# Odd columns of the odd rows from half the table columns, after a turn of the pairs

## The chip, the core and the metric

The kernel runs on one core of a Trainium2 chip. The metric is the device time of one execution in microseconds (us). Three runs of the kernel before gave 1187.96, 1188.49 and 1189.62 us; the median is 1188.49 us. The engines are named as the profile names them: PE is TensorE's matmul, PEld its weight load, DVE is VectorE, ACT is ScalarE, POOL is GpSimd, SP is SyncE, which issues most transfers.

## The reference

```python
x: (8, 3136, 256)      w_in: (256, 1024)   conv_w: (3, 1024)   w_out: (1024, 256)     # float32

X = np.fft.fft(np.fft.fft(x, axis=1), axis=2).real          # FNet mixing: sequence, then features
h = np.maximum(X @ w_in, 0.0)
c = conv_w[0] * h[s-1] + conv_w[1] * h[s] + conv_w[2] * h[s+1]   # along the sequence, zeros outside
out = (h * sigmoid(c)) @ w_out
```

## The kernel before, in words

**The two halves of a batch.** For each of the 8 batches the kernel first makes the Fourier transform along the sequence of the 256 features, as two matrices `PQ[b]` (`pt`, the cosine part, and `qt`, the sine part) of 128 folded features by 1569 frequencies. Then it walks over 32 steps, (chunk of frequencies c, block of 128 hidden features f): 4 chunks by 8 blocks. Over all batches that is 256 steps. The loop at the end of the file is written out by hand as a software pipeline: in cycle t it emits the sigmoid of step t-2, the two products and their copies of step t+1, the sums, seeds and first tap of steps t and t+2, the other taps of step t-1, the gate of step t-2 and the second matrix product of step t-3. Every engine runs its instructions in the order in which they are emitted.

**A step.** `products` (PE, tiles `pb` and `pa`) multiplies `qt` and `pt` with `G`, the input weights that already hold the feature transform. `copies` (ACT, L708) brings `pb` to SBUF, `combine` (DVE, L719) makes sum and difference, `first_tap` (ACT, L725) and `tap` (DVE, L730, twice) are the convolution, `sigmoid` (ACT, L745) and `gate` (half POOL L753, half DVE L754) make the gated rows `g`, and `mm2` (PE, tile `po`) multiplies them with `wout`.

**The transform of the next batch** is slipped into the steps of the present one. It has two kinds of work. `fold_ops(b)` (DVE, L156 to L194, with small copies on POOL, L178) adds and subtracts mirrored rows of `x`, and mirrored features, until four things are left: even and odd frequencies, each for cosine and sine. The result is `wt[b][0]` (even) and `wt[b][1]` (odd), of 98 or 99 partitions by 4 components by 4 row groups q by 128 features. There are 14 such operations in a batch, 7 for each half h of the row groups. `units(b)` then holds nine matrix products against the tables `tabs` (cosine and sine, 393 or 392 frequencies wide): `odd_even` and `odd` for odd frequencies, `even_even` and `even` for even ones, each for sn = 1 (`qt`) and sn = 0 (`pt`), and `feature` for one row in batch 0. A unit is matmuls into one PSUM bank (`pd`, or a spare bank in batch 0), perhaps a copy of it by ACT (`copy`, L294, L324) and sums on DVE (`fin`). `odd` takes row groups 0 and 2, the odd rows: 4 matmuls of 392 columns, no copy, and two sums of 392 elements that read the bank (L340, L342).

**Where things stand.** `side` is a table of extra work by cycle and place ("act", "dve", "pe", "pool", "load"); `at(cycle, where, fn)` fills it. `ends` says until which cycle each batch's folds are spread; the units of batch b follow from `ends[b]` on, and the last folds (batch 7) lie in cycles 157 to 188, the last units in 189 to 220. A unit's `copy` stands in the "act" place of a cycle, which is after `copies` of the next step, and its `fin` in the "dve" place of the same cycle, which is between the two taps.

**The start.** Before the first cycle, batch 0 goes through the same work at once. SP issues the loads of `x`, then the odd tables (`load_tables(1)`, L227 to L233), a quarter of `w_in`, the even tables (`load_tables(0)`), the feature tables `dm` and the rest of `w_in`. PE runs eight products of no use (`keep_on`, into `pb` and `pa`) until the tables are there, then the four odd units of batch 0 in four rounds, part by part. ACT makes the negated tables that the sine terms need (`mirror_tables`, L247) and halves one row (`mend_row`, L241). DVE turns the weights from 64 to 32 bits (`narrow`, L543 to L561).

Of the kernel before, what the change touches and what calls it, by code (L numbers as in the profile page):

```python
# [36 lines left out]
def kernel(  # L37
# [103 lines left out]
    def fold_ops(b):  # L141
# [4 lines left out]
        def half(h):  # L146
# [60 lines left out]
        (o0, s0), (o1, s1) = half(0), half(1)  # L207
        return o0 + o1, {**s0, **{len(o0) + j: f for j, f in s1.items()}}

    tabs = [const.tile([P, n, HQ, HE], F32, name="tab%d" % n) for n in (2, 4)]
    PQ, eb, er = {}, {}, {}
    ed = edp.tile([B, (RC // 2 + 1) * RC], F32, name="ed")

    def table(k, st, q, cols):
        return tabs[st // 2][0:k, st, q, cols] if st < 2 else tabs[1][0:k, st - 2, q, cols]

    def load_tables(par):


        st = slice(2 * par, 2 * par + 2)
        to = tabs[par][:, 0:2].rearrange("p s q i -> p s (q i)")
        n = HQ * HE
        m = NP // 2 // 16 * 16
        for i in range(2):
            nc.sync.dma_start(out=to[i:2 * m:2], in_=dft_seq[0:m, st, HQ * i:HQ * (i + 1)]  # L227
                              .rearrange("p s q i -> p s (q i)"))
        assert NP == 2 * m + 2
        nc.sync.dma_start(out=to[2 * m:NP], in_=bass.AP(  # L230
            tensor=dft_seq.tensor, offset=dft_seq.offset + (m * 4 + 2 * par) * NQ * HE,
            ap=[[n, 2], [NQ * HE, 2], [1, n]]))
        nc.sync.dma_start(out=to[NP:KR], in_=bass.AP(  # L233
            tensor=dft_seq.tensor, offset=dft_seq.offset + ((NP * 4 + 2 * par) * NQ - HQ + 2) * HE,
            ap=[[n, 1], [NQ * HE, 2], [1, n]]))

    def mend_row(par, half):

        for st in range(2):
            row = tabs[par][96:NP, st, HQ - 1]  # L240
            act(row, row, AF.Copy, scale=half[96:NP])  # L241

    def mirror_tables(q):

        for to, of, s in ((2, 1, -1.0), (3, 0, 1.0)):
            for i in range(2):
                act(tabs[1][0:KR, to, q:q + 2, i:HO:2], tabs[1][0:KR, of, q:q + 2, i:HO:2], AF.Copy,  # L247
                    scale=-s if i else s)

    class Unit:  # L250
# [11 lines left out]
        def part(self, i):  # L262
            if i == 0:
                self.p = spare()
            self.mms[i](self.p)

# [13 lines left out]
    def units(b):  # L280
# [34 lines left out]
        def stat(sn):  # L315
            return ((w(4 + 2 * sn), 2 + sn), (w(5 + 2 * sn), 4 + sn))
# [480 lines left out]
    nc.gpsimd.memset(PQ[0][1][96:P, :], 0.0)  # L797
    for f in fold_ops(0)[0]:
        f()
# [49 lines left out]
    def at(cycle, where, fn):  # L849
        side.setdefault((cycle, where), []).append(fn)  # L850
# [57 lines left out]
    for b in range(1, B):  # L908
        ops, singles = fold_ops(b)
        c0, n = ends[b - 1], ends[b] - ends[b - 1]  # L910
        if b == 1:

            cs = [c for c in range(4, ends[1] + 1) if c not in taken]
            assert len(cs) == len(ops) and cs[7] > NF + 4
        else:
            cs = [free(c0 + j * n // len(ops)) for j in range(len(ops))]
            assert cs[-1] < ends[b]
        if b + 1 < B:
            for h in range(2):
                for j, fn in enumerate(load_ops(b + 1, h, nc.sync)):  # L920
                    at(cs[7 * h + 6] + 1 + j, "load", fn)
# [112 lines left out]
```

## Time and profile before

| what | value |
|---|---|
| runs of the kernel before | 1187.96, 1188.49, 1189.62 us |
| span of the profiled execution | 1184.7 us |
| median of the runs less that span | 3.8 us |
| instructions in it | 15354 |

The profile is of one execution. Its span runs from the first instruction of the core to the last one; what lies around it, 3.8 us against the median, is not in the trace, and is taken as the same for both kernels. A row of a group reads: line, engine, operation, tiles out<-in, shapes, count, then busy time and mean duration of one in ns, then the idle time of the engine just before. A float32 matmul stands as two records, so a unit of 4 matmuls shows as x8. On DVE and ACT an instruction's record starts before the one before it has ended, so the distance from start to start, and not the duration, is what one costs when the engine is full.

### The profile page before, as it was taken

How to read it: one execution, taken by the hardware profiler on the slowest of the kernel's cores; microseconds unless marked ns; L12 is line 12 of the kernel's file. 1: busy time of each engine (PE TensorE's matmuls, PEld its weight loads, DVE VectorE, ACT ScalarE, POOL GpSimd, SP SyncE). 2: the span in 40 equal slices, each digit the busy share in tenths (PEclk: the TensorE clock that was granted, in tenths of full speed). 3: DMA queues.
4: the chain of work that ended last, by engine and by line, in shares of the span. 5: the costliest groups of instructions: out<-in, count | busy, mean ns of one | idle time of the engine just before them, and what ended most of it. 6: DMA issues, size and time to landing. Idle time of an engine off the chain costs nothing.

```text
span 1184.7 us, 15354 instructions
## 1 busy us (share of the span) xinstructions
PE 1158.7 (98%) x4820; PEld 891.6 (75%) x4820; DVE 1128.7 (95%) x1633; ACT 886.7 (75%) x1888; POOL 407.6 (34%) x476
## 2 busy tenths in 40 slices
PE   4999999999999999999999999999999999999998
PEld 2667777777777777777777777777777777777776
DVE  7899999999999999999998999999998898999996
ACT  2578668777777778877777877877777777888885
POOL 5225443433434342424333232432322232222222
PEclk9999999999999999999999999999999999999999
DMA  9803233121212021202131110310010100100000
GB/s 226 195 10 107 57 55 89 49 69 41 72 38 86 28 77 52 83 7 76 34 96 46 48 48 14 104 34 27 27 34 21 32 27 27 51 31 27 28 27 32
DMA packets 70068, 66.08 MB, mean 56 GB/s; under 512 B 28107, under 2 KB 57683, under 8 KB 69987
## 3 DMA queue, kind: packets, MB, share of 16 engines
q1 hardware_dynamic: 64349, 51.98, 15.6%
q0 software_dynamic: 5120, 12.85, 3.7%
q8 instruction: 38, 0.62, 0.2%
q14 instruction: 43, 0.35, 0.1%
q10 hardware_dynamic: 518, 0.28, 0.1%
HBM read 39.33 MB, written 25.74 MB: 55 GB/s over the span
## 4 chain that ended last, share of the span: by engine, by line
PE 89%; DVE 7%; issue 1%; POOL 1%; ACT 1%; DMA 0%; DVEq 0%; SPq 0%; POOLq 0%; ACTq 0%
PE po L92 54%; PE pb L92 14%; PE pa L92 13%; PE pd L92 8%; DVE g L730 3%; DVE h L719 1%; DVE g L754 1%; POOL xh L131 1%; DVE raw L558 0%; DVE xh L167 0%; DVE wout L551 0%; ACT os L778 0%; DVE w L194 0%; DVE win L551 0%; DMA out_dram<-os 0%
## 5 line engine op out<-in xcount | busy, mean ns | idle before, releaser
L92 PE MATMUL po<-wout,g 128*128 128x256 f32 x3072 | 706.1, 379 | 4.2 <-DVE g L754 4.2
L92 PEld LDWEIGHTS po<-wout,g 128*128 128x128 f32 x3072 | 580.8, 190 | 148.7 <-issue 20.0
L730 DVE SCALAR_TENSOR_TENSOR g<-h,cw,g 128x770 f32<-128x770 f32 (+1 forms) x512 | 575.7, 1124 | 5.7 <-ACT g L725 2.1
L753 POOL TENSOR_TENSOR g<-g,h 128x385 f32<-128x385 f32 (+2 forms) x256 | 270.4, 1057 | 721.1 <-ACT g L745 542.1
L708 ACT ACTIVATE nb<-pb 128x386 f32<-128x386 f32 (+2 forms) x494 | 219.9, 500 | 168.2 <-PE pb L92 167.5
L745 ACT ACTIVATE g<-g 128x385 f32<-128x385 f32 (+4 forms) x512 | 244.8, 531 | 81.8 <-DVE g L730 78.4
L719 DVE CUSTOM_DVE_ANT_0 h<-pa,nb 128x386 f32<-128x386 f32 (+2 forms) x503 | 260.0, 556 | 2.5 <-POOL h L686 2.5
L725 ACT ACTIVATE g<-h,cw 128x770 f32<-128x770 f32 (+1 forms) x256 | 244.2, 954 | 0.0
L92 PE MATMUL pb<-qt,G 127*128 127x387 f32 (+2 forms) x512 | 213.7, 498 | 0.9 <-ACT G L641 0.9
L92 PE MATMUL pa<-pt,G 128*128 128x387 f32 (+2 forms) x512 | 211.8, 494 | 0.0
L672 ACT ACTIVATE pa<-eb,ge 128x387 f32<-128x387 f32 (+2 forms) x256 | 155.2, 607 | 0.6 <-ACT ft L477 0.6
L92 PEld LDWEIGHTS pa<-pt,G 128*128 128x128 f32 x512 | 96.9, 189 | 73.5 <-issue 18.0
L754 DVE TENSOR_TENSOR g<-g,h 128x385 f32<-128x385 f32 (+2 forms) x256 | 147.7, 577 | 2.4 <-ACT g L745 2.4
L92 PE MATMUL pd<-tab,w 98*128 98x196 f32 (+3 forms) x448 | 115.9, 356 | 0.0
L92 PEld LDWEIGHTS pb<-qt,G 127*128 127x128 f32 x512 | 91.5, 190 | 18.8 <-ACT G L641 1.9
L131 POOL DMA_INDIRECT xh<-in_x_dram,idx x64 | 99.8, 1560 | 13.0 <-issue 10.6
L92 PEld LDWEIGHTS pd<-tab,w 98*128 98x128 f32 (+1 forms) x448 | 82.7, 191 | 12.6
L778 ACT COPY os<-po 128x256 f32<-128x256 f32 x196 | 57.6, 397 | 6.6 <-PE po L92 3.3
L156 DVE TENSOR_TENSOR xh<-xh 98x1020 f32<-98x1020 f32 (+1 forms) x32 | 40.4, 1265 | 2.6 <-DMA xh<-in_x_dram,idx 2.6
L167 DVE TENSOR_TENSOR xh<-xh 98x1024 f32<-98x1024 f32 (+1 forms) x32 | 40.5, 1266 | 0.1
L178 POOL COPY w<-xh 98x4 f32<-98x4 f32 (+1 forms) x32 | 24.2, 758 | 6.1 <-DVE xh L167 3.6
L193 DVE TENSOR_TENSOR w<-xh 98x508 f32<-98x508 f32 (+1 forms) x32 | 23.0, 720 | 0.1
(124 smaller groups left out, 330.3 us busy)
## 6 DMA issues: line engine op xcount, KB each, us to landing
out_dram<-os SPq DMA_DIRECT2D x192, 128.0 KB
xh<-in_x_dram SPq DMA_DIRECT2D x16, 784.0 KB
eb<-ed SPq DMA_DIRECT2D x16, 193.5 KB
tab<-dft_seq_dram SPq DMA_DIRECT2D x4, 589.5 KB
raw<-in_moe_w_in_dram SPq DMA_DIRECT2D x4, 512.0 KB
raw<-in_moe_w_out_dram SPq DMA_DIRECT2D x1, 2048.0 KB
eb<-ed SPq DMA_DIRECT2D x8, 209.0 KB
eb<-ed SPq DMA_DIRECT2D x7, 193.0 KB
```

The costliest lines, as they stand in the source:

```text
L92: nc.tensor.matmul(o, l, r, start=start, stop=stop, skip_group_check=True)
L131: nc.gpsimd.indirect_dma_start(out=xh[b, h][0:NP, 7 - m].rearrange("p q d -> p (q d)"), out_offset=None, in_=bass.AP(tensor=x.tensor, offs ...
L167: vt(flat(to, to + 2), flat(0, 2), flat(2, 4), op=op)
L672: act(pa[s][:, 0:n], eb[b, c], AF.Copy, scale=ge[:, f:f + 1])
L708: act(nb[s][:, i, cols], p[:, cols], AF.Copy, scale=-1.0 if i else 1.0)
L719: nc.vector._custom_dve(TENSOR_ADD_SAT, out=to, in0=a[:, cols], in1=c[:, i, cols], s0=BIG, s1=0.0)
L725: act(gs[s], hs[s][:, 0:n], AF.Copy, scale=cw[:, 0, s[2]:s[2] + 1])
L730: stt(out=g, in0=h[:, k:k + n], scalar=cw[:, k, f:f + 1], in1=g, op0=ALU.mult, op1=ALU.add)
L745: act(gs[s][:, c], gs[s][:, c], AF.Sigmoid)
L753: gt(g[:, p], g[:, p], h[:, p], op=ALU.mult)
L754: vt(g[:, v], g[:, v], h[:, v], op=ALU.mult)
L778: nc.scalar.copy(out=osb[:, j % 2], in_=pt[:, j % 2])
```

## The change

The units `odd` no longer multiply with the 392 columns of the odd tables. An odd frequency is 4j+1 or 4j-1, so the rows are first turned, pair by pair, by the angle of frequency 1; after that both frequencies come from the products at frequency 4j, as sum and difference of the cosine part and the sine part. So a unit makes 197 columns of each part, side by side in one bank, with every second column of the even tables, and the sums follow.

- **The turn.** In batches 1 to 7, two ACT operations for each half copy the two sides of the odd rows of `wt[b][1]` with the sine as scale (`scaled`, tile `rt`, 98 partitions by 256), and two DVE operations turn them in place (`turned`, 98 by 256). They are one more fold operation for each half: 16 in a batch, and `ends[1]` goes from 20 to 22. In batch 0 ACT makes four scaled copies for each half (8 in all), and the unit adds them up with 8 matmuls.
- **The unit.** 4 matmuls of 197 columns (8 in batch 0) in place of 4 of 392. ACT copies one half of the bank (`copy`, 197 columns). DVE makes two more sums of 196 elements into an SBUF tile, and the two sums of 392 now read that tile and not the bank.
- **The tables.** Of the odd tables only row groups 1 and 3 at 196 columns are loaded (`load_odd`, 8 transfers with rows of 784 bytes, in place of 4 with rows of 6288 bytes), then the even tables (`load_even`), and only after these the first quarter of `w_in`. `load_turn` (4 transfers of single elements on ACT's queue) brings the cosines and sines of the turn. `mirror_tables` is 4 ACT operations of 196 elements, where it was 8 of 392.

```diff
@@ fold_ops, half(h)
+            def sides():
+                w = wt[b][1][0:NP, :, 2 * h]
+                return w[:, 0:4:2], w[:, 1:4:2]
+            made = []
+            def scaled():
+                if b == 0:
+                    a, c = sides()
+                    for i, (v, k) in enumerate(((a, 0), (c, 2), (a, 1), (c, 0))):
+                        if i % 2 == 0:
+                            parted[h, i // 2] = rp.tile([P, 2, 2, P], F32, name="rt", tag="rt")
+                        act(parted[h, i // 2][0:NP, i % 2], v, AF.Copy, scale=turn[0:NP, k, h:h + 1])
+                    return
+                made.append(rp.tile([P, 2, 2, P], F32, name="rt", tag="rt"))
+                for i, v in enumerate(sides()):
+                    act(made[0][0:NP, i], v, AF.Copy, scale=turn[0:NP, 1, h:h + 1])
+            def turned():
+                if b == 0:
+                    return
+                for i, v in enumerate(sides()):
+                    stt(out=v, in0=v, scalar=turn[0:NP, 0, h:h + 1], in1=made[0][0:NP, 1 - i],
+                        op0=ALU.mult, op1=ALU.add if i else ALU.subtract)
-            ops = [pair(0), pair(2), both(6, ALU.subtract), feats(1), both(4, ALU.add), evens, feats(0)]
-            return ops, {3: single(1), 6: single(0)}
+            ops = [pair(0), pair(2), both(6, ALU.subtract), feats(1), both(4, ALU.add), turned, evens, feats(0)]
+            return ops, {3: single(1), 7: single(0)}, {5: scaled}
@@ tables
-    tabs = [const.tile([P, n, HQ, HE], F32, name="tab%d" % n) for n in (2, 4)]
+    tabs = [const.tile([P, 2, HQ, HE], F32, name="tab2"), const.tile([P, 4, 2, QO], F32, name="tab4")]
+    turn = const.tile([P, 3, 2], F32, name="turn")
+    rp = ctx.enter_context(tc.tile_pool(name="rp", bufs=4))
+    def load_odd(eng):
+        def at_(p, s, q):
+            return dft_seq.offset + ((p * 4 + 2 + s) * NQ + q) * HE
+        for s in range(2):
+            for i in range(2):
+                eng.dma_start(out=tabs[1][i:2 * MR:2, s], in_=bass.AP(
+                    tensor=dft_seq.tensor, offset=at_(0, s, HQ * i + 1),
+                    ap=[[4 * NQ * HE, MR], [2 * HE, 2], [1, QO]]))
...
@@ units, odd(sn)
-            prods = [(q, wf, st) for q in (0, 2) for wf, st in stat(sn)]
-            mms = [product((slice(0, P), slice(0, HO)), wf, st, q, slice(0, HO), i == 0, i == 3)
-                   for i, (q, wf, st) in enumerate(prods)]
+            n = HE // 2 + 1
+            def from_(i, e):
+                if b == 0:
+                    return lambda k, q: parted[q // 2, i ^ sn][0:k, e, sn, :]
+                return w(4 + 2 * sn + (i ^ sn))
+            m = 1 if b else 2
+            mms = [product((slice(0, P), slice(i * n, (i + 1) * n)), from_(i, e), i, q,
+                           slice(0, HE, 2), i + q + e == 0, q == 2 and e == m - 1)
+                   for q in (0, 2) for i in range(2) for e in range(m)]
+            def copy(p):
+                a_["s", sn], a_["b", sn] = [asp.tile([P, HO + 2], F32, name="as", tag="as") for _ in range(2)]
+                nc.scalar.copy(out=a_["s", sn][:, 0:n], in_=p[:, n:2 * n])
             def fin(p):
-                a, bb, t = a_[sn][:, 0:HO], p[:, 0:HO], PQ[b][sn]
+                a, t = a_[sn][:, 0:HO], PQ[b][sn]
+                u, v, bb = p[:, 0:n], a_["s", sn][:, 0:n], a_["b", sn][:, 0:HO]
+                if sn:
+                    vt(bb[:, 0:HO:2], v[:, 0:n - 1], u[:, 0:n - 1], op=ALU.add)
+                    vt(bb[:, 1:HO:2], v[:, 1:n], u[:, 1:n], op=ALU.subtract)
+                else:
+                    vt(bb[:, 0:HO:2], u[:, 0:n - 1], v[:, 0:n - 1], op=ALU.subtract)
+                    vt(bb[:, 1:HO:2], u[:, 1:n], v[:, 1:n], op=ALU.add)
                 vt(t[:, 1:Q4 + 1:2], a, bb, op=ALU.add)
                 x0, x1 = (bb, a) if sn else (a, bb)
                 vt(t[:, M - 1:Q4:-2], x0, x1, op=ALU.subtract)
-            return Unit(b, mms, lambda p: None, fin)
+            return Unit(b, mms, copy, fin)
@@ the start
+    load_turn(nc.scalar)
+    act(turn[0:NP, 2], turn[0:NP, 1], AF.Copy, scale=-1.0)
     nc.gpsimd.memset(tabs[1][0:1, 0, 0, 0:1], 0.0)
-    load_tables(1)
+    load_odd(nc.sync)
+    load_even()
     w_in[0].load(nc.sync)
-    load_tables(0)
     nc.sync.dma_start(out=dm, in_=dft_dim[:, :, 0:2])
...
-    mirror_tables(0)
     mend_row(1, half)
-    mirror_tables(2)
+    mirror_tables()
@@ the schedule
-    ends = [9, 20, per + 12] + [per * (b - 1) - 3 + max(11 - 4 * (b - 2), 0) for b in range(3, B)]
+    ends = [9, 22, per + 12] + [per * (b - 1) - 3 + max(11 - 4 * (b - 2), 0) for b in range(3, B)]
...
+        for j, fn in pres.items():
+            at(cs[j], "act", fn)
```

More of the change, by code (lines that the diff above doesn't have):

```diff
@@ L202, in feats @@
                 return f
[L204 to L212 removed]
+            def sides():
[21 more added lines that the diff above has]
+            return ops, {3: single(1), 7: single(0)}, {5: scaled}
+        parts = [half(h) for h in range(2)]
+        n = len(parts[0][0])
+        return (parts[0][0] + parts[1][0],
+                *[{n * h + j: f for h in range(2) for j, f in parts[h][i].items()} for i in (1, 2)])
+    parted = {}
+    tabs = [const.tile([P, 2, HQ, HE], F32, name="tab2"), const.tile([P, 4, 2, QO], F32, name="tab4")]
+    turn = const.tile([P, 3, 2], F32, name="turn")
+    rp = ctx.enter_context(tc.tile_pool(name="rp", bufs=4))
     PQ, eb, er = {}, {}, {}
@@ L216, in table, with load_even @@
     def table(k, st, q, cols):
[L217 to L223, printed above, removed]
+        if st < 2:
+            return tabs[0][0:k, st, q, cols]
+        return tabs[1][0:k, st - 2, q // 2, cols]
+    MR = NP // 2 // 16 * 16
+    assert NP == 2 * MR + 2
+    def load_even():
+        to = tabs[0].rearrange("p s q i -> p s (q i)")
@@ L237, in mend_row, with load_turn @@
+    def load_turn(eng):
+        for s in range(2):
+            for i in range(2):
+                eng.dma_start(out=turn[i:NP:2, s].unsqueeze(2), in_=bass.AP(
+                    tensor=dft_seq.tensor, offset=dft_seq.offset + ((2 + s) * NQ + HQ * i) * HE,
+                    ap=[[4 * NQ * HE, NP // 2], [2 * HE, 2], [1, 1]]))
     def mend_row(par, half):
         for st in range(2):
-            row = tabs[par][96:NP, st, HQ - 1]
+            row = tabs[0][96:NP, st, HQ - 1] if par == 0 else tabs[1][96:NP, st, 1]
@@ L264, in part @@
                 self.p = spare()
-            self.mms[i](self.p)
+            n = len(self.mms) // 4
+            for f in self.mms[i * n:(i + 1) * n]:
+                f(self.p)
         def copy(self):
@@ L797 @@
     nc.gpsimd.memset(PQ[0][1][96:P, :], 0.0)
-    for f in fold_ops(0)[0]:
+    ops, _, pres = fold_ops(0)
+    for j, f in enumerate(ops):
+        if j in pres:
+            pres[j]()
         f()
@@ L908 @@
     for b in range(1, B):
[L909 removed]
+        ops, singles, pres = fold_ops(b)
         c0, n = ends[b - 1], ends[b] - ends[b - 1]
@@ L913 @@
             cs = [c for c in range(4, ends[1] + 1) if c not in taken]
-            assert len(cs) == len(ops) and cs[7] > NF + 4
+            assert len(cs) == len(ops) and cs[len(ops) // 2] > NF + 4
         else:
@@ L920 @@
                 for j, fn in enumerate(load_ops(b + 1, h, nc.sync)):
-                    at(cs[7 * h + 6] + 1 + j, "load", fn)
+                    at(cs[len(ops) // 2 * (h + 1) - 1] + 1 + j, "load", fn)
         for j, fn in enumerate(ops):
```

18 lines of the change are left out of this document (10 added, 8 removed).

## The prediction

> **What bounds the kernel now.** I read the page first: its busy line, then its chain of work that ended last.
>
> ```profile
> PE 1158.7 (98%) x4820; PEld 891.6 (75%) x4820; DVE 1128.7 (95%) x1633; ACT 886.7 (75%) x1888; POOL 407.6 (34%) x476
> ...
> PE 89%; DVE 7%; issue 1%; POOL 1%; ACT 1%; DMA 0%; DVEq 0%; SPq 0%; POOLq 0%; ACTq 0%
> ```
>
> TensorE is the bound, but VectorE is three points behind it, and the change takes work from the one and gives some to the other. A mean over the span can't decide that, so the next view is the windows, with columns for PE, PEld, DVE, ACT and POOL. I cut them where the work changes: 60 to 160 (folds of batch 1), 160 to 880 (folds of batches 2 to 7), 880 to 1025 (units of batch 7 alone), the rest (neither).
>
> ```profile
> 60.00:160.00 100.00, 96.81 (x400) 71.77 (x399) 99.38 (x149) 74.20 (x169) 40.31 (x49) 1.00 0.28 60
> 160.00:400.00 240.00, 239.37 (x1000) 183.81 (x999) 235.69 (x345) 181.72 (x387) 95.41 (x107) 1.00 0.21 61
> 400.00:880.00 480.00, 479.58 (x2005) 373.02 (x2004) 466.85 (x688) 370.92 (x778) 164.44 (x189) 1.00 0.15 48
> 880.00:1025.00 145.00, 145.00 (x608) 113.22 (x607) 131.16 (x184) 111.03 (x239) 40.65 (x41) 1.00 0.10 31
> 1025.00:1150.00 125.00, 125.00 (x514) 97.11 (x513) 123.94 (x161) 104.45 (x221) 31.64 (x40) 1.00 0.09 30
> ```
>
> In the first window VectorE bounds (99.38 of 100, PE 96.81). From 160 to 1150 TensorE is never idle for more than 0.7 us in a window. VectorE's idle time is 4.3 us in the second window and 13.2 in the third. The last row warns: there VectorE has neither folds nor units and still shows 99%. Its busy time stretches, which the taps show, same shape, in 100 to 160, 160 to 400, 400 to 880 and 1030 to 1150 (count, busy us, mean ns):
>
> ```profile
> L730 DVE SCALAR_TENSOR_TENSOR g<-h,cw,g 128x770 f32<-128x770 f32 x26 | 26.5, 1018 | 0.0
> L730 DVE SCALAR_TENSOR_TENSOR g<-h,cw,g 128x770 f32<-128x770 f32 x75 | 79.7, 1062 | 0.3
> L730 DVE SCALAR_TENSOR_TENSOR g<-h,cw,g 128x770 f32<-128x770 f32 x169 | 182.8, 1082 | 0.8
> ...
> L730 DVE SCALAR_TENSOR_TENSOR g<-h,cw,g 128x770 f32<-128x770 f32 x48 | 58.5, 1218 | 0.8
> ```
>
> The more room VectorE has, the longer a tap: 1018 ns where VectorE bounds, 1218 where it has least to do. So part of VectorE's busy time is slack, and it goes when VectorE gets tight. That decides this case.
>
> **What TensorE saves.** The timeline of PE has a whole `odd` unit of today, and an `even` unit of 197 columns with every second column of a table, just the form that `odd` gets:
>
> ```profile
> 141.04 2.80 PE L92 MATMUL pd<-tab,w 98*128 98x392 f32 x8
> 143.68 0.81 PE L92 MATMUL pb<-qt,G 127*128 127x387 f32 x2
> ...
> 156.38 1.56 PE L92 MATMUL pd<-tab,w 98*128 98x197 f32 x8
> 157.78 0.87 PE L92 MATMUL pb<-qt,G 127*128 127x418 f32 x2
> ```
>
> From start to next start: 143.68 - 141.04 = 2.64 us before, 157.78 - 156.38 = 1.40 after. Saved are 1.24 us a unit, 2.48 a batch, 17.4 us over 14 units of batches 1 to 7. In batch 0 there are 8 matmuls: 2.80 against 2.64, 0.16 more for each of two units.
>
> **What VectorE gets.** Sums of 196 elements with one input in PSUM exist; turns of 256 elements don't, but one operation of their kind of 128 elements and one of 512 do.
>
> ```profile
> 948.45 0.36 DVE L300 TENSOR_TENSOR as<-pd,as 128x196 f32<-128x196 f32 x1
> 948.73 1.01 DVE L730 SCALAR_TENSOR_TENSOR g<-h,cw,g 128x770 f32<-128x770 f32 x1
> ```
>
> ```profile
> 5.83 0.28 DVE L561 SCALAR_TENSOR_TENSOR cw<-raw,cw 24x128 f32<-24x128 f32 x1
> ...
> 60.33 0.69 DVE L561 SCALAR_TENSOR_TENSOR wout<-raw,wout 128x512 f32<-128x512 f32 x1
> ```
>
> A sum costs 948.73 - 948.45 = 0.28 us from start to start. A turn lasts between 0.28 and 0.69, by the straight line 0.42; less the 0.08 by which such records overlap it is 0.34, and with a scalar from memory a little more: I take 0.38. A batch has 4 turns and 4 new sums: 1.5 + 1.1 = 2.6 us. The two sums of 392 remain as they are; only their second input moves from PSUM to SBUF.
>
> **What that makes of each window.** By the cycles of the schedule, 400 to 880 holds 3.7 batches of turns and 3.8 pairs of odd units, 160 to 400 2.3 and 1.7, 60 to 160 1 and 0.5, 880 to 1025 none and 1.
>
> *400 to 880.* TensorE: -3.8 x 2.48 = -9.4, so 470.6. VectorE: 466.9 + 3.7 x 1.5 + 3.8 x 1.1 = 476.6 busy as it stands; but if its 225 taps (the 169 of the row and the wider ones of every fourth chunk, taken alike) go back from 1082 to 1018 ns, 14.4 us go: 462.2. That leaves 8.4 us of idle time, where it has 13.2 now. TensorE remains the bound if VectorE's waits shrink. I take 2.4 us off for places where they don't: **-7**. *160 to 400.* TensorE 240 - 1.7 x 2.48 = 235.8; VectorE 235.7 + 2.3 x 1.5 + 1.7 x 1.1 = 241.0, less 44 ns (1062 - 1018) on half as many taps is 236.1. Both bound; with 1.4 us of idle time it is 237.5: **-2.5**. *60 to 160.* VectorE bounds, so its additions count in full, 1.5 + 0.6: **+2.1**, and TensorE's saving is lost. *880 to 1025.* No folds; one batch of odd units, VectorE has 14 us: TensorE's 2.5, **-2.4**. *After that* nothing changes: 0.
>
> What else hides: ACT gets 4 scaled copies and 2 bank copies a batch.
>
> ```profile
> L294 ACT COPY as<-pd 128x197 f32<-128x197 f32 x14 | 4.6, 331 | 0.0
> L247 ACT ACTIVATE tab<-tab 99x392 f32<-99x392 f32 x8 | 3.9, 573 | 15.5 <-DMA tab<-dft_seq_dram 15.5
> ```
>
> Between 0.33 (197) and 0.57 (392) a copy of 256 is 0.40, so 4 x 0.40 + 2 x 0.33 = 2.3 us on an engine that is 75% busy: nothing by itself, but DVE waits for each result, and the seed and first tap stand behind them in ACT's queue. POOL and the steady transfers are unchanged.
>
> Some of the stretch comes from POOL, as the timeline shows at one place: two taps and a gate of POOL that start together, and an undisturbed gate.
>
> ```profile
> 603.87 2.79 DVE L730 SCALAR_TENSOR_TENSOR g<-h,cw,g 128x832 f32<-128x832 f32 x2
> 603.88 1.90 POOL L753 TENSOR_TENSOR g<-g,h 128x448 f32<-128x448 f32 x1 [3.50 <-ACT g L745]
> ...
> 607.40 0.98 POOL L753 TENSOR_TENSOR g<-g,h 128x448 f32<-128x448 f32 x1 [1.62 <-ACT g L745]
> ```
>
> The gate takes 1.90 where it takes 0.98 alone. [...]
>
> **The start.** SP's issues, ACT's first use of the odd tables, PE's change from idle products to the odd units, and DVE's first sum:
>
> ```profile
> 13.41 1.40 SPq L227 DMA_DIRECT2D tab<-dft_seq_dram  x2
> 14.86 0.44 SPq L230 DMA_DIRECT2D tab<-dft_seq_dram  x1
> 15.34 0.68 SPq L233 DMA_DIRECT2D tab<-dft_seq_dram  x1
> ```
>
> ```profile
> 22.52 1.97 ACT L247 ACTIVATE tab<-tab 99x392 f32<-99x392 f32 x4 [15.46 <-DMA tab<-dft_seq_dram]
> ```
>
> ```profile
> 24.00 1.88 PE L92 MATMUL pa<-w 98*128 98x512 f32 x4
> 25.72 2.48 PE L92 MATMUL po<-tab,w 98*128 98x196 f32 x10
> ```
>
> ```profile
> 32.55 0.36 DVE L328 TENSOR_TENSOR as<-as,po 128x196 f32<-128x196 f32 x1 [2.42 <-ACT as L324]
> ```
>
> Loading a quarter of the odd tables gains nothing, for `odd` now needs the even ones, which are issued behind eight small transfers: 2 x 1.40 + 2 x 0.44 + 2 x 0.68 = 5.0 us, so from 18.4 to 20.9. Today the last odd table is issued by 16.0 and used at 22.52, 6.5 later: the even ones land at 27.4 by that, and no later, since part of these 6.5 us was `x` still loading. The idle products hold PE until 25.72 in any case. So the odd units start between 0 and 1.7 us late; I take 0.7. Then come 0.3 us of matmuls in batch 0 and four new sums on DVE, 1.1 us, in a row that is unbroken from the first sum on. A quarter of `w_in` lands later, but DVE idles 2.42 us ahead of 32.55, which covers it. **+2**, between 1.1 and 3.5.
>
> **Sum:** +2 + 2.1 - 2.5 - 7 - 2.4 = -7.8. Span 1184.7 - 7.8 = 1176.9. The median of the runs, 1188.49, is 3.8 us over the profiled span, so 1180.7 us.
>
> **Rivals.**
>
> *A: VectorE becomes the bound from 60 to 880, through its waits for ACT (slower).* A unit's bank copy stands in ACT's queue behind `copies` of the next step, which waits for PE. The waits of 400 to 900, in total us, times, longest:
>
> ```profile
> DVE as L328 <- ACT as L324: 5.2, 5, 2.1
> DVE as L298 <- ACT as L294: 4.8, 8, 1.1
> ```
>
> 10.0 us for 13 waits, 0.77 each. The change adds four such waits a batch (two turns, two odd units): 15 x 0.77 = 11.6 us in 400 to 880, 8 x 0.77 = 6.2 in 160 to 400. If the old and the new ones all stay, 400 to 880 is 462.2 + 13.2 + 11.6 = 487 (+7), 160 to 400 is 236.1 + 4.3 + 6.2 = 246.6 (+6.6), and the sum is +2 + 2.1 + 6.6 + 7 - 2.4 = +15.3, so 1203.8 us. These are 35.3 us of waits, of which the forecast keeps 12.2; the kernel turns slower than before from the point where 7.8 of the other 23.1 stay, a third. Against it speaks a window in which VectorE bounds today:
>
> ```profile
> 220.00:240.00 20.00, 19.49 (x79) 14.94 (x80) 19.93 (x31) 15.00 (x31) 5.37 (x10) 1.00 0.01 4
> ```
>
> VectorE's idle time there is 0.07 us: where PE isn't late, ACT isn't either. But no unit lies in it. Chance 0.20.
>
> *B: it evens out.* The stretch of the taps goes only half: 400 to 880 is 462.2 + 7.2 + 10.8 = 480.2, 160 to 400 236.1 + 2.5 + 1.4 = 240.0, and the sum is +2 + 2.1 + 0 + 0.2 - 2.4 = +1.9; with somewhat fewer waits 0: 1188.5 to 1190.4. For it: in 160 to 400, with VectorE at 98%, taps still take 1062. Chance 0.16.
>
> *C: nearly all of TensorE's saving arrives.* 160 to 400 -4.2, 400 to 880 -9.4, start +1.1: with +2.1 and -2.4 the sum is -12.9, 1175.6. Chance 0.18.
>
> *D: the halved columns don't halve the time.* If a record of 197 columns cost what a weight load does (891.6 us for 4820, 185 ns, so 1.48 for eight), 14 x 0.08 = 1.1 us of the saving would go. The row at 156.38 has the very form at 1.40: inside the forecast.
>
> **How the numbers follow.** Forecast 0.46 (1177 to 1185), C 0.18, B 0.16, A 0.20. Two tenths of a per cent, 2.4 us, is what a measurement of this kernel can tell from no change. Faster: forecast, C and a little of B, 0.66. Within: most of B and the lowest part of A, 0.14. Slower: the rest of A, and of B, 0.20. The range takes in C and the lower half of A: 1174 to 1196.
>
> **What would show each step.** The `pd` unit of 197 columns with `w` of the odd half at 1.40 us from start to start; turns near 0.38; PE with idle time in 60 to 160 and 160 to 400, and next to none in 400 to 880; mean tap of 400 to 880 near 1020 to 1040; `po<-tab` of the odd units starting between 25.7 and 27.4; stages after 1025 as long as before. It is wrong if DVE's waits for `as` and `rt` in 400 to 880 exceed 12 us, or the taps stay at 1080 there, or the start is over 4 us late.

## The result, and the profile after

| | time, median (range) | span of the profiled execution, granted clock |
|---|---|---|
| before, 5 runs | 1188.04 us (1185.01 to 1189.62) | 1184.7 us, 0.998 |
| changed kernel, 5 runs | 1200.36 us (1193.45 to 1201.21) | 1193.2 us, 0.995 (a run of 1194.98) |

The ratio is 1.0089 with a 95% interval of 1.0063 to 1.0115. The kernel became slower where 1180.7 us was forecast, and lies above the range, 1174 to 1196. Its runs are 7.8 us apart, and they go with the granted clock: 1193.45 and 1194.98 had 0.997 and 0.995, the other three 0.988 to 0.990. That belongs to the result, as the start below shows.

From the page of the changed kernel, the busy line and the chain of work that ended last:

```profile
PE 1152.5 (97%) x4836; PEld 890.9 (75%) x4836; DVE 1134.9 (95%) x1693; ACT 899.6 (75%) x1937; POOL 405.5 (34%) x476
...
PE 72%; DVE 16%; issue 4%; ACT 4%; DMA 2%; POOL 1%; SPq 0%; DVEq 0%; ACTq 0%; POOLq 0%
```

TensorE is 6 us less busy, though the odd units alone save 17. VectorE is 6 us busier. TensorE's share of the chain fell from 89 to 72%, VectorE's rose from 7 to 16%: the bound has moved towards VectorE. The windows of the prediction:

```profile
60.00:160.00 100.00, 94.33 (x388) 69.65 (x389) 96.17 (x143) 76.73 (x175) 47.25 (x45) 1.00 0.30 54
160.00:400.00 240.00, 234.73 (x985) 178.51 (x985) 235.41 (x361) 178.93 (x385) 92.87 (x106) 1.00 0.22 61
400.00:880.00 480.00, 477.56 (x2022) 373.43 (x2020) 472.04 (x722) 379.47 (x809) 159.89 (x189) 1.00 0.16 50
880.00:1025.00 145.00, 145.00 (x617) 114.32 (x616) 133.64 (x195) 113.62 (x242) 39.25 (x44) 1.00 0.09 29
1025.00:1150.00 125.00, 125.00 (x516) 97.32 (x515) 123.41 (x163) 105.22 (x224) 30.82 (x39) 1.00 0.11 32
```

TensorE, idle 0.6 us from 160 to 400 and 0.4 from 400 to 880 before, is now idle 5.3 and 2.4. From 880 on it is full again. What it waits for, from 60 to 880 (us in total, times, longest), first of the matmuls, then of the weight loads, then of the weight loads of the kernel before:

```profile
PE po L92 <- DVE g L830: 10.2, 22, 1.2
```

```profile
PEld po L92 <- DVE g L830: 47.3, 79, 1.8
```

```profile
PEld po L92 <- DVE g L754: 15.6, 24, 1.5
```

The second product waits for the last operation of VectorE's step three times as often as before. So VectorE now bounds a part of this stretch. It isn't full either: from 160 to 880 it is idle for 12.5 us and TensorE for 7.7, each waiting at times for the other.

Stages can be compared without fixed windows by the start of the first matmul of `mm2` (`po<-wout,g`) of a step. How much later it comes than in the profile of the kernel before, and what was forecast for the stretch from the row above to this one:

| step | before, us | after, us | later by | of it in this stretch | forecast |
|---|---|---|---|---|---|
| 0 | 63.0 | 71.0 | +8.0 | +8.0 | +2 |
| 24 | 180.1 | 189.8 | +9.8 | +1.8 | +2.1 |
| 72 | 394.6 | 408.2 | +13.6 | +3.8 | -2.5 |
| 184 | 883.7 | 894.6 | +10.9 | -2.7 | -7 |
| 216 | 1025.2 | 1033.6 | +8.4 | -2.5 | -2.4 |
| 240 | | | +8.4 | 0 | 0 |

Two places failed: the start, and the steps 24 to 184, where -9.5 was forecast and +1.1 came.

**The start.** SP's issues, PE and ACT of the changed kernel:

```profile
13.49 1.37 SPq L274 DMA_DIRECT2D tab<-dft_seq_dram  x2
15.31 0.70 SPq L277 DMA_DIRECT2D tab<-dft_seq_dram  x1
16.06 0.61 SPq L279 DMA_DIRECT2D tab<-dft_seq_dram  x1
18.12 1.27 SPq L274 DMA_DIRECT2D tab<-dft_seq_dram  x2
...
22.59 0.62 SPq L264 DMA_DIRECT2D tab<-dft_seq_dram  x1
```

```profile
25.84 0.49 PE L92 MATMUL po<-tab,w 98*128 98x196 f32 x2
29.90 1.65 PE L92 MATMUL po<-tab,rt 98*128 98x197 f32 x4 [3.56 <-DMA tab<-dft_seq_dram]
...
35.49 0.86 PE L92 MATMUL po<-tab,rt 98*128 98x197 f32 x4
...
42.79 0.88 PE L92 MATMUL pd<-tab,ea 99*1 99x197 f32 x16 [2.29 <-issue]
```

```profile
41.73 0.33 ACT L403 COPY as<-po 128x197 f32<-128x197 f32 x1 [1.51 <-DVE qt L416]
42.08 1.13 ACT L294 ACTIVATE tab<-tab,half 2x393 f32<-2x393 f32 x2
```

```profile
SPq L274 <- DMA tab<-dft_seq_dram: 1.4, 1, 1.4
```

SP stands still between 16.67 and 18.12; the waits of SP give the reason, the landing of an earlier table. So the last even table is issued at 23.2, not 20.9. It is used 6.7 us later, which is the 6.5 of the prediction. So PE, which had begun the odd units at 25.84, waits 3.56 us for the even tables. It waits a second time, 2.29 us, ahead of the feature unit: that needs the halved row of the even tables (L294), which stands in ACT's queue behind the odd units' bank copies, and the last of these waits 1.51 us for a buffer (`as`) that VectorE frees.

In the first gap, 1.9 us after it began, the granted clock falls. The window 30 to 35 of the changed kernel has PEclk 0.50, where before it is 1.00:

```profile
30.00:35.00 5.00, 5.00 (x16) 5.00 (x17) 3.50 (x7) 0.00 (x0) 0.00 (x0) 0.50 0.97 352
```

In all, the clock is at half for 6.8 us from 28.2 and 3.4 us from 52.1; before, only for 3.4 from 42.3, with no gap of TensorE over 0.5 us in the 26 us ahead of it. A round of four records takes 1.65 us at half clock (29.90) and 0.86 at full (35.49). The gap need not be 3.56 us long: in two runs below rounds at half clock (1.65 and 1.52 us) also follow the first gap, which is 2.87 us in e6 and 1.99 in e4. After the 1.19 us of e9 the rounds take 0.86.

### The profile page after: what moved, and what is told of

Its sections match the earlier page's. It is cut to its first block, busy times and chain, and to the rows that moved or that the text cites. A ratio compares the mean times of both kernels' runs of the same rounds, so it can differ in the third digit from the quotient of the medians.

```text
span 1193.2 us, 15532 instructions
## 1 busy us (share of the span) xinstructions
PE 1152.5 (97%) x4836; PEld 890.9 (75%) x4836; DVE 1134.9 (95%) x1693; ACT 899.6 (75%) x1937; POOL 405.5 (34%) x476
## 4 chain that ended last, share of the span: by engine, by line
PE 72%; DVE 16%; issue 4%; ACT 4%; DMA 2%; POOL 1%; SPq 0%; DVEq 0%; ACTq 0%; POOLq 0%
PE po L92 46%; PE pb L92 11%; PE pa L92 10%; DVE g L806 7%; PE pd L92 5%; DVE h L795 3%; DVE g L830 2%; POOL xh L131 1%; DMA tab<-dft_seq_dram 1%; ACT nb L784 1%; ACT g L821 1%; DMA out_dram<-os 1%; ACT os L854 1%; DVE w L194 1%; DMA xh<-in_x_dram 0%
## 5 line engine op out<-in xcount | busy, mean ns | idle before, releaser
L806 DVE SCALAR_TENSOR_TENSOR g<-h,cw,g 128x770 f32<-128x770 f32 (+1 forms) x512 | 564.8, 1103 | 4.1 <-ACT g L801 0.9
L829 POOL TENSOR_TENSOR g<-g,h 128x385 f32<-128x385 f32 (+2 forms) x256 | 265.1, 1036 | 727.5 <-ACT g L821 550.2
L92 PE MATMUL pd<-tab,w 98*128 98x197 f32 (+2 forms) x448 | 98.5, 318 | 1.0 <-DVE w L194 1.0
L178 POOL COPY w<-xh 98x4 f32<-98x4 f32 (+1 forms) x32 | 26.9, 842 | 7.3 <-DVE xh L172 3.7
```

The source lines that it names most:

```text
L92: nc.tensor.matmul(o, l, r, start=start, stop=stop, skip_group_check=True)
L806: stt(out=g, in0=h[:, k:k + n], scalar=cw[:, k, f:f + 1], in1=g, op0=ALU.mult, op1=ALU.add)
L829: gt(g[:, p], g[:, p], h[:, p], op=ALU.mult)
```

## The experiments

Each row gives the time, its ratio to the kernel before on the same chip, and from the profile the lateness of step 0 and what the stretch from step 24 to step 184 gained (-) or lost (+) against the kernel before.

| run | time, us | ratio [95%] | step 0 | 24 to 184 |
|---|---|---|---|---|
| changed kernel | 1200.36 | 1.0089 [1.0063, 1.0115] | +8.0 | +1.1 |
| e1 even tables first | 1194.85 | 1.0067 [1.0053, 1.0081] | +8.2 | +0.6 |
| e2 PE kept busy | 1195.98 | 1.0072 [1.0059, 1.0086] | +5.2 | 0.0 |
| e9 start reordered | 1189.73 | 1.0017 [1.0008, 1.0025] | +1.8 | +0.8 |
| e3 no turn | 1190.59 | 1.0013 [0.9997, 1.0029] | +13.6 | -4.5 |
| e4 no sums | 1186.48 | 0.9991 [0.9981, 1.0] | +5.7 | -4.6 |
| e5 neither | 1179.85 | 0.993 [0.9918, 0.9942] | +6.5 | -8.4 |
| e6 scaled copies early | 1197.04 | 1.0059 [1.0037, 1.0082] | +13.5 | -1.6 |
| e7 POOL 5/8 of the gate | 1227.41 | 1.0309 [1.0284, 1.0334] | +14.6 | +23.3 |
| e10 e9, POOL 3/8 | 1192.0 | 1.0038 [1.0024, 1.0052] | +2.3 | +2.1 |
| e11 before, POOL 3/8 | 1188.62 | 1.0009 [1.0, 1.0018] | -0.1 | 0.0 |
| e12 e9 and e6 | 1186.24 | 0.9992 [0.9983, 1.0001] | +3.4 | -1.0 |
| e13 e12, bank copies first | 1181.04 | 0.9937 [0.9923, 0.995] | +2.2 | -5.9 |
| e14 before, bank copies first | 1189.25 | 1.0005 [0.9996, 1.0014] | +0.4 | +1.0 |

The same steps 24 to 184 in the changed kernel, e1, e2 and e9, whose edits touch only the start, spread from 0.0 to 1.1; that is the grain of the last column.

### The start: e1, e2, e9

e1 issues the even tables ahead of the odd ones.

```diff
-    nc.gpsimd.memset(tabs[1][0:1, 0, 0, 0:1], 0.0)
-    load_odd(nc.sync)
+    nc.gpsimd.memset(tabs[0][0:1, 0, 0, 0:1], 0.0)
     load_even()
+    load_odd(nc.sync)
```

> The changed kernel, with the even tables issued ahead of the eight small transfers of the odd ones. Theory S (most of the loss is the start: the odd units of batch 0 wait for the even tables, which are issued late): the first second matrix product (po<-wout) starts at 63 to 66 us instead of 71.0, the odd units of batch 0 start near 25.8 instead of 29.9, PE has no idle gap there and no stretch at half clock between 28 and 35 us, and the time is 5 to 9 us under that of the changed kernel, so 1186 to 1193. Rival V (the loss is VectorE's load in the steps, the start is only moved slack): the time stays within 2 us of 1195 to 1200.

PE in e1:

```profile
26.30 0.57 PE L92 MATMUL po<-tab,w 98*128 98x196 f32 x2 [1.02 <-DMA tab<-dft_seq_dram]
...
37.14 0.88 PE L92 MATMUL pd<-tab,ea 99*1 99x197 f32 x16 [2.33 <-ACT tab L294]
37.95 9.03 PE L92 MATMUL po<-tab,w 99*128 99x99 f32 x32
```

The late tables are gone: the odd units start at 26.30, at full clock, and the feature unit 5.7 us earlier than in the changed kernel. Yet step 0 comes as late as there. After the idle 2.33 us the clock falls to half for 17.1 us, from 37.9 on, and the even units take 9.03 us where they take 4.85. The miss shows that the clock is a cost of its own.

e2 leaves the loads and has PE run four more idle products ahead of the odd units.

```diff
+    keep_on([idle] * 4)
```

> The changed kernel, with four more idle products on PE ahead of the odd units of batch 0, so that PE is busy while it waits for the even tables; loads as they are. If the granted clock falls to a half because PE sat idle 3.6 us (26.3 to 29.9), the clock stays whole through the odd units of batch 0, which then take 8 us instead of 10.6, and the first second matrix product starts 3 to 4 us earlier, at 67 to 68 us. If the half clock has another cause, or the delay is only that of the tables, it starts at 71 as before. Rival V: no change in the time beyond 2 us either way.

In the profiled run (1191.13 us) the clock is whole through the odd units, and step 0 comes 5.2 us late in place of 8.0. So 6.8 us of half clock cost 2.8 us, 0.41 us each. The other runs, at clocks of 0.992 to 0.994, took 1195.2 to 1196.4. The second gap, ahead of the feature unit, is still there, and e1 shows what can follow it; no trace of these slower runs exists.

e9 is e1 with the halving of the row moved ahead of the odd units.

```diff
     mirror_tables()
+    mend_row(0, half)
     for i in range(4):
...
-    mend_row(0, half)
```

> The start alone, put in another order: even tables before the odd ones (as in the run before), and the halving of the even tables' row ahead of the odd units in ACT's queue, so that the feature unit does not wait behind the odd units' copies. Theory C (the start cost 8 us: some 2.6 of work, some 2.6 of late tables, the rest by TensorE's idle times and the half clock that follows them): TensorE's idle time before the feature unit shrinks from 2.3 us to under 1, no half clock longer than 3.4 us follows, the first mm2 of step 0 comes 2 to 4 us after that of the kernel before, in place of 8, and the time is 1188 to 1191. Rival N (the start's loss is the work itself, the clock no more than a companion): step 0 comes 6 us or more late again, 1193 or more.

```profile
26.17 0.57 PE L92 MATMUL po<-tab,w 98*128 98x196 f32 x2 [1.19 <-DMA tab<-dft_seq_dram]
...
34.61 0.87 PE L92 MATMUL pd<-tab,ea 99*1 99x197 f32 x16
35.41 4.85 PE L92 MATMUL po<-tab,w 99*128 99x99 f32 x32
...
43.40 1.05 PE L92 MATMUL po<-dm,win 128*128 128x1 f32 x6 [1.80 <-DVE win L635]
```

The gap ahead of the odd units is 1.19 us in place of 3.56, and the one ahead of the feature unit is gone. A later one of 1.80 us has come, for VectorE's conversion of the weights. The half clock is 3.4 us, as before. Step 0 comes 1.8 us late, and the time is 1189.73 us; each against the kernel before on its chip, that is 9 to 10 us less than the changed kernel. So in this order the change costs the start 1.8 us; the order that it came with costs the rest. How much that is depends on the clock: 6.2 us in the profiled run of the changed kernel; the profile of e6 below, which has the same start, shows 6.8 and then 17.1 us of half clock and step 0 at +13.5, at a granted clock of 0.990, which is that of the changed kernel's slower runs. None of these was profiled, so for the median this is likely and not shown.

### What VectorE got: e3, e4, e5

e3 leaves out the turn in batches 1 to 7, scaled copies and VectorE's operations; e4 the two new sums and the bank copy of each odd unit, so that the sums of 392 read the bank; e5 both.

```diff
@@ e3: scaled(), turned()
+                if b:
+                    return
...
-                if b == 0:
-                    return
+                return
@@ e4: copy(p), fin(p) of odd
-                nc.scalar.copy(out=a_["s", sn][:, 0:n], in_=p[:, n:2 * n])
+                pass
...
-                u, v, bb = p[:, 0:n], a_["s", sn][:, 0:n], a_["b", sn][:, 0:HO]
+                a, t, bb = a_[sn][:, 0:HO], PQ[b][sn], p[:, 0:HO]
```

> The changed kernel with the turn left out in batches 1 to 7: neither ACT's scaled copies nor VectorE's turns run there (the odd frequencies of these batches are not those of the reference). Theory V (VectorE has no room between 60 and 880 us): 28 turns of some 0.40 us are 11 us less on VectorE, and the time falls by 5 to 10 us; steps 24 to 184 take 4 to 9 us less. Rival (TensorE bounds, the turns are hidden): less than 2 us. Rival A (the waits for ACT's results cost the time): 5 us, the 4.9 us that VectorE waits for rt.

> The changed kernel with the two new sums of each odd unit and ACT's copy of half the bank left out, in all batches; the sums of 392 read the bank as it stands (the odd frequencies are not those of the reference). Theory V: 28 sums of 0.28 us are 8 us less on VectorE in the steps and 1 us less in the start, and the time falls by 4 to 8 us. Rival (TensorE bounds): less than 2 us, all of it in the start.

> The changed kernel without the turn of batches 1 to 7 (its ACT copies and DVE operations) and without the two new sums and the bank copy of each odd unit: both parts are left out, so that only TensorE's halved columns remain. Theory V (VectorE bounds 160 to 880, so what VectorE gets counts in full there): from the first mm2 of step 24 to that of step 184 the changed kernel lost 1.1 us, without the turn it gained 4.5, without the sums 4.6; the two add up, so without both it gains 9.5 to 11.5. Rival S (VectorE's instructions stretch, and either part alone already gives back what there is): no more than 6. Rival W (TensorE's saving is smaller than its columns say): no more than 6 too, but then DVE has idle time there and TensorE none. If V and the start costs what it did in the four runs so far (5 to 8): 1181 to 1185 us.

Against +1.1, the turn costs 5.6 us between step 24 and step 184 and the sums 5.7; together 9.5. Rows of the changed kernel, 400 to 880, give the sizes:

```profile
L226 DVE SCALAR_TENSOR_TENSOR w<-w,turn,rt 98x256 f32<-98x256 f32 x16 | 7.0, 482 | 2.4 <-ACT rt L220 2.4
...
L409 DVE TENSOR_TENSOR as<-as,pd 128x196 f32<-128x196 f32 x4 | 1.4, 357 | 0.3 <-ACT as L403 0.2
L410 DVE TENSOR_TENSOR as<-as,pd 128x196 f32<-128x196 f32 x4 | 1.4, 352 | 0.0
```

Less 0.08 us of overlap, a turn costs 0.40 (0.38 was taken) and a sum 0.28 (0.28). With the prediction's 6 batches of turns and 5.5 of odd units from 160 to 880 that is 6 x 4 x 0.40 = 9.6 us and 5.5 x 4 x 0.28 = 6.2. Left out alone, they give 5.6 and 5.7 us back, and left out together 9.5 of the 15.8 us. So what VectorE gets counts for the greater part, and not in full. The stretch with neither is -8.4, not the -13.6 of TensorE alone (5.5 pairs of units by 2.48); e5 expected 9.5 to 11.5. Halved columns, not missing work, are all that is left in e5, but VectorE still waits for ACT's bank copies of the other units (160 to 880):

```profile
DVE as L354 <- ACT as L350: 6.7, 10, 0.9
DVE as L384 <- ACT as L380: 5.3, 7, 1.2
```

That made me try the waits.

### The waits: e6, e12, e13, e14

VectorE's waits in the changed kernel, 60 to 890:

```profile
DVE w L226 <- ACT rt L220: 4.9, 11, 2.0
DVE as L383 <- ACT as L379: 2.3, 3, 1.1
...
DVE as L412 <- ACT as L403: 1.3, 2, 0.8
DVE as L409 <- ACT as L403: 0.8, 2, 0.5
```

In the kernel before, over the same stretch:

```profile
DVE as L298 <- ACT as L294: 7.1, 11, 1.1
DVE as L328 <- ACT as L324: 6.5, 8, 2.1
```

9.3 us, against 13.6 before. At first I took them for harmless. e6 puts the scaled copies one fold operation earlier in ACT's queue.

```diff
-            ... {5: scaled}
+            ... {4 if b else 5: scaled}
```

> The scaled copies of the turn stand one fold operation earlier in ACT's queue in batches 1 to 7, so that DVE has them long before it turns. Theory V: DVE waited for them only 4.9 us in all, in 11 waits, and part of that is hidden: step 24 to step 184 within 1.5 us of the changed kernel, and the time within 2 us of it at the same granted clock. Rival A of the prediction (the new waits are the loss): the stretch gets shorter by 4 us or more.

VectorE's wait for `rt` goes to nothing, and the stretch is 2.7 us shorter: more than the 1.5 that I allowed and less than rival A's 4. e12 repeats it on e9's start, and there it is 1.8 us (+0.8 to -1.0).

> The reordered start, and the scaled copies of the turn one fold operation earlier. Alone, the earlier copies made 24 to 184 2.7 us shorter and DVE's waits for them went from 2.9 us to 0. With the start, step 0 comes 1.8 us after that of the kernel before, 24 to 184 takes 0.8 to 2 us less than before, 184 to 216 2.5 less: 1186 to 1188. If the 2.7 were the half clock's making in that one profile, the time stays at 1189 to 1191.

e13 then takes the remaining waits away: the units' bank copies go ahead of the step's own work in ACT's queue, and e14 does this to the kernel before.

```diff
-            at(cs[i + 1], "act", u.copy)
+            at(cs[i + 1], "first", u.copy)
```

> The reordered start, the scaled copies one fold operation earlier, and the units' bank copies ahead of the step's own products and copies in ACT's queue (place "first" of the cycle in place of "act"). Theory V: VectorE bounds from 24 to 184, so its last waits for ACT there (2.9 us for L379, 2.4 for L403, 11 in all with the copies of the other units hidden in part) count nearly in full: DVE's waits for as fall under 1.5 us, 24 to 184 is 2 to 5 us shorter than with the start and the scaled copies alone (which was 1.0 us shorter than the kernel before), 1181 to 1185 us. Rival W (each such wait is covered by PE's own lateness): within 1 us of 1186.2. Rival Q (the copy now holds up the step's nb copy, for which the products' bank and combine wait): slower by 1 us or more.

> The kernel before with its bank copies in the same place. There DVE waits 13 us for as from 160 to 880, but TensorE bounds and is idle 1.0 us in these 720. Theory V: within 1 us of the kernel before, 1186.5 to 1188. If waits of VectorE cost even where TensorE bounds: 2 us or more less.

VectorE's waits from 160 to 880 in e13, and the windows 160 to 400 and 400 to 880:

```profile
DVE h L795 <- POOL h L762: 3.1, 4, 1.0
DVE as L383 <- ACT as L379: 0.2, 1, 0.2
```

```profile
160.00:400.00 240.00, 236.87 (x1001) 182.36 (x1000) 238.16 (x365) 184.76 (x398) 93.27 (x107) 1.00 0.22 64
400.00:880.00 480.00, 479.22 (x2037) 377.49 (x2036) 477.17 (x728) 384.88 (x816) 166.34 (x187) 1.00 0.16 48
```

The stretch is another 4.9 us shorter, and the whole kernel takes 1181.04 us: it beats both, by 0.63% the one before (0.50 to 0.77%). In e14 the waits for bank copies go too (0.2 us left of 13.2 from 160 to 880; 3.3 us for TensorE come instead), and the time stays. Its window:

```profile
400.00:880.00 480.00, 479.86 (x2006) 373.35 (x2005) 475.90 (x688) 370.45 (x779) 174.88 (x188) 1.00 0.15 48
```

VectorE is 9 us busier there with as many instructions (466.85 before): in this window, where TensorE bounds, the time freed on VectorE turned into longer operations. (From 160 to 400 it did not, 234.73 us against 235.69.) So these waits cost nothing in the kernel before. In the changed one they count in full: from e9 to e13 VectorE's waits for ACT's scaled and bank copies, from 160 to 880, go from 6.4 us to 0.2, and the stretch gets 6.7 us shorter.

### The taps: e7, e10, e11

The prediction had read the stretched taps as slack. Rows of taps of 770 in the changed kernel, 100 to 160, 160 to 400, 400 to 880 and 1030 to 1150:

```profile
L806 DVE SCALAR_TENSOR_TENSOR g<-h,cw,g 128x770 f32<-128x770 f32 x27 | 28.7, 1065 | 0.0
L806 DVE SCALAR_TENSOR_TENSOR g<-h,cw,g 128x770 f32<-128x770 f32 x72 | 74.3, 1032 | 0.1
L806 DVE SCALAR_TENSOR_TENSOR g<-h,cw,g 128x770 f32<-128x770 f32 x174 | 182.9, 1051 | 0.6
L806 DVE SCALAR_TENSOR_TENSOR g<-h,cw,g 128x770 f32<-128x770 f32 x48 | 58.5, 1218 | 0.8
```

They fell by 30 and 31 ns in the middle two, where 44 and 64 were forecast. In the first, where VectorE bounded already, they rose from 1018 to 1065, and not by the added work alone: e5, without it, has 1047 there. e7, e10 (on e9) and e11 (on the kernel before) change POOL's part of the gate.

```diff
-        m = n - n // (4 if third(steps.index(s) + 2) else 2)
+        m = n - n // 4 if third(steps.index(s) + 2) else n - n * 5 // 8
```

(e10 and e11: `n * 3 // 8`.)

> The changed kernel with POOL taking 5/8 of the gate in place of a half, outside the steps where it has a quarter: DVE's gate gets 112 elements of 448 shorter... that is 336 of 896 in place of 448. Theory V (VectorE bounds): DVE's gate is some 0.1 us a step shorter, of the 160 steps between 24 and 184 the most have this share, so 24 to 184 gets 4 to 10 us shorter and the time 5 to 12 us less than the changed kernel's at the same granted clock. [...] Rival P: POOL's gate of 5/8 ends later than DVE's and mm2 waits for POOL: longer by 2 us or more.

> The reordered start of the last call, and POOL taking 3/8 of the gate in place of a half. With 5/8 DVE's gate was 0.10 us shorter (451 ns in place of 554), but each of the two taps of a step 0.14 longer (1184 in place of 1045), 0.18 a step in all, and 24 to 184 took 22 us more. Theory V with the taps' stretch made by POOL: the other way round, the taps get shorter by up to 0.1 us each and DVE's gate 0.1 longer, VectorE wins 0.05 to 0.1 a step, and 24 to 184 is 5 to 14 us shorter than with a half (TensorE's own saving ends it at some 13); time 1176 to 1185. Rival L (the taps' stretch is VectorE's slack, as the prediction had it): taps as before, DVE's gate 0.1 us longer in 160 steps, so 8 to 16 us more: 1198 to 1206.

> The same share of 3/8 in the kernel before. Theory V: TensorE bounds it (idle 0.6 us from 160 to 400 and 0.4 from 400 to 880), so shorter taps bring at most what TensorE's idle time and the first 160 us hold: 0 to 4 us less, 1184 to 1188. Rival L: VectorE gets 0.1 us a step more, and has 13 us of idle time in 400 to 880 but 4 in 160 to 400: 2 to 8 us more.

Tap and gate on VectorE from 160 to 880, in the changed kernel, in e7 and in e10:

```profile
L806 DVE SCALAR_TENSOR_TENSOR g<-h,cw,g 128x770 f32<-128x770 f32 x245 | 256.1, 1045 | 0.8
...
L830 DVE TENSOR_TENSOR g<-g,h 128x385 f32<-128x385 f32 x122 | 67.6, 554 | 1.4 <-ACT g L821 1.4
```

```profile
L806 DVE SCALAR_TENSOR_TENSOR g<-h,cw,g 128x770 f32<-128x770 f32 x233 | 275.8, 1184 | 0.7
...
L830 DVE TENSOR_TENSOR g<-g,h 128x289 f32<-128x289 f32 x117 | 52.8, 451 | 0.0
```

```profile
L806 DVE SCALAR_TENSOR_TENSOR g<-h,cw,g 128x770 f32<-128x770 f32 x244 | 249.4, 1022 | 0.8
...
L830 DVE TENSOR_TENSOR g<-g,h 128x482 f32<-128x482 f32 x122 | 79.8, 654 | 0.0
```

With 96 elements more on POOL, VectorE's gate is 0.10 us shorter and each of the two taps 0.14 us longer: VectorE is the bound and gets slower, and the stretch loses 22 us more. POOL's gate itself got only 0.12 us longer (1111 against 990 ns from 160 to 880, both its shapes), so the size of the taps' stretch stays unexplained. Rival P had the sign, but not the mechanism (from 160 to 880 the matmuls wait 17.1 us for VectorE's gate, and only 0.2 us of a weight load's wait are for POOL's), and no theory the size. (The expectation's 336 of 896 elements was wrong; the rows show 289 in place of 385.) The other way, a tap wins 0.02 and the gate loses 0.10: the stretch loses 1.3 us against e9, where e10 expected a gain of 5 to 14. So POOL's share of the gate, which runs beside the taps, is one thing that sets their length (1184, 1045 and 1022 ns at 5/8, a half and 3/8), and of the three shares tried a half is the best. It isn't the only one: at an unchanged share the rows above run from 1032 to 1218 ns. In the kernel before, where TensorE bounds, 3/8 leaves the stretch as it was (e11: 0.0 us).

## Why the prediction was wrong, point by point

- **The start, "+2, between 1.1 and 3.5": wrong, +8.0 in the profiled execution.** With the right order the size would have been near (e9: +1.8). The failed step is "the odd units start between 0 and 1.7 us late; I take 0.7". Most of these units had to wait until 29.90, 4.2 us after 25.72. The sum of issue times, 5.0 us for eight transfers, left out that the second four would have to wait for a landing; 7.3 us passed from the first to the end of the eighth. And two things were not in the sum at all: that the feature unit's table row stands in ACT's queue behind the new bank copies, and that PE, after its idle time, went on at half clock. "Over 4 us late" was named as what would make the prediction wrong. It was: 6 of the 16.3 us by which the profiled span (1193.2 against 1176.9) missed, and probably more in the median. That e9 comes out at +1.8 is no proof of the terms: its own gap of 1.80 us is in none of them.
- **60 to 160, "+2.1": the number is right, +1.8 up to step 24, and by luck.** The working was that VectorE's additions count in full, 2.1 us, and "TensorE's saving is lost". But e5, which has the halved columns without the additions, gains 2.1 us from step 0 to step 24 (+6.5 to +4.5, before rounding), so the saving isn't lost; and what VectorE got costs 3.9 us there. A part of these 3.9 is the longest wait for `rt`, 2.0 us: e6 and e12, which are without it, have +1.0 in this stretch.
- **160 to 880, "-2.5" and "-7": wrong, +3.8 and -2.7.** The failed step is "if its 225 taps go back from 1082 to 1018 ns, 14.4 us go". They went back to 1051, so 225 x 31 ns = 7.0 us went; from 160 to 400 about 111 taps lost 30 ns and not 44, 3.3 in place of 4.9. These two terms are 9.0 us too favourable, of the 10.6 by which the sum missed here. Beside them, VectorE's idle time from 400 to 880 is 480 - 472.04 = 8.0 us, where the forecast had 8.4 and 2.4 more for its waits, but from 160 to 400 it is 4.6, not 1.4. Put right, 400 to 880 is 476.6 - 7.0 + 8.0 = 477.6 us, 2.4 less than the 480, against the 2.7 measured: there the way of adding up holds. For 160 to 400 it gives 241.0 - 3.3 + 4.6 = 242.3, 2.3 more than the 240, against the 3.8 measured; 1.5 us stay open (half of them go if the 32 wide taps, which lost 7 ns each, are taken apart).
- **What the taps showed.** "The more room VectorE has, the longer a tap" was a correlation between windows. e13 breaks it: VectorE's idle time from 400 to 880 is down to 2.8 us, and its taps are no shorter than the changed kernel's 1051 ns:

```profile
L806 DVE SCALAR_TENSOR_TENSOR g<-h,cw,g 128x770 f32<-128x770 f32 x172 | 181.7, 1056 | 0.7
```

  So the stretch is not slack that VectorE gives up when it gets tight. e7 and e10 move the taps by POOL's share of the gate. Why the taps got 31 ns shorter at an unchanged share is open: e5, with none of VectorE's new work, has 1036 and 1056 in the two windows, so it isn't the added work that shortens them. That the gate meets the taps less often when TensorE's steps are shorter would fit, but wasn't tried.
- **Rival A, the waits: its price was wrong, its mechanism half right.** It expected up to 35 us; 9.3 are there from 60 to 890. But they count in full, as e12 and e13 show (-1.8 and -4.9). Its point of decision was a third of 23 us; with the taps as they came out, there was no room left for any.
- **Rival B, "the stretch of the taps goes only half": right on the taps of 400 to 880** (31 of 64 ns; from 160 to 400 it was 30 of 44). Its +0.2 for 160 to 880 lies near the +1.1 by luck: it had 0 and +0.2 where +3.8 and -2.7 came. With the start at +8 its sum is +7.9, a span of 1192.6 against the 1193.2 measured, and that agreement is luck too.
- **Rival C, all of TensorE's saving:** its sum is -12.8, not -12.9. Even without VectorE's new work (e5), 8.4 us come from 160 to 880 and not its 13.6.
- **The sums of 392 and the turns: near enough.** The sums of 392, whose second input came from PSUM before and comes from SBUF now, took 0.57 us from 160 to 880 against 0.56 before, and a turn cost 0.40 against the 0.38 taken: over 28 of each some 0.8 us more in all.
- **880 to 1025, "-2.4", and nothing after: right**, -2.5 and 0. A unit has the forecast size, 160.87 - 159.47 = 1.40 us from start to start (the second record is the next product):

```profile
159.47 1.56 PE L92 MATMUL pd<-tab,w 98*128 98x197 f32 x8
160.87 0.81 PE L92 MATMUL pb<-qt,G 127*128 127x387 f32 x2
```

- **What lies around the span** was taken as 3.8 us from a median; the changed kernel's profiled run has 1194.98 - 1193.2 = 1.8.

## What to carry to other kernels

Where two engines are within a few per cent, ask of each window what the second engine can really give up: a stretched operation is slack only if an experiment says so; here POOL's gate, beside the taps, set a part of their length (e7: 1184 ns against 1045). When the bound moves to an engine, its old waits, which cost nothing, can begin to cost their whole length (6.2 us less of them from e9 to e13, 6.7 us less of the stretch), so move what it waits for ahead in the queue in the same edit; here that and the order of the start made 1181.04 us out of 1200.36. In a start, count for every table when it lands, and for every small operation what stands in front of it in its queue.

## What the runs showed of the hardware

- A gap of TensorE of 2.3 us, ahead of the feature unit, was followed within 1 us by half clock in e1 and e6 (17.1 us each) and in e3 and e7, where the even units took 9.03 and 9.02 us in place of 4.85, but not in the changed kernel or in e2, with gaps of 2.29 us, where the next half clock of 3.4 us came some 9 us later. What decides that stays open here.
- The half clock in the start costs 0.41 us for each us (e2 against the changed kernel); e6 against the changed kernel, with 13.7 us more of it and step 0 5.5 us later, gives 0.40. The changed kernel's runs differ by 0.65% and go with the granted clock (1193.45 us at 0.997, 1201.21 at 0.988).
- A gate of POOL with a quarter more elements (481 against 385) made the taps of VectorE that run beside it 13% longer (1184 against 1045 ns).
- VectorE's busy time is elastic: with as many instructions from 400 to 880, 688, it was 466.85 us in the kernel before and 475.90 in e14, at the same time per execution.
